# Sparse attention with a gated convolution: the same operations of one TensorE-bound kernel in another fixed order

## Chip, cores and metric

The kernel runs on 1 core of one Trainium2 chip. The metric is the time of one execution on the device in microseconds (us), the median of several runs. A core has five engines, each with its own instruction stream that it works off strictly in order: TensorE (PE in the profile; its weight loads are PEld), VectorE (DVE), ScalarE (ACT), GpSimd (POOL) and SyncE (SP). Here SyncE issues all DMAs. The engines meet through semaphores alone: an instruction waits until what it reads is written, and until what it overwrites has been read.

## The reference, cut to what matters

There are 8 batches of 8 heads with 576 tokens and head width 64. Heads 0 to 3 attend locally (the 32 tokens up to their own), heads 4 to 7 to every 32nd token up to their own. The result, 512 wide per token, goes through a gated projection.

```python
scores = q @ k.T / 8                       # per batch and head
rel = pos[:, None] - pos[None, :]
mask_local = (rel >= 0) & (rel < 32)                          # heads 0..3
mask_strided = (rel >= 0) & (pos[None, :] % 32 == pos[:, None] % 32)   # heads 4..7
attn = softmax(where(mask, scores, -1e9));  x = attn @ v      # x: (8, 576, 512)
gate = sigmoid(sum(conv_w[k] * shifted(x, 4 - k) for k in range(5)))
out = (gate * (x @ w_val)) @ w_out
```

## The kernel before, in words

Each batch b goes through these steps; their names are those of the groups in the code.

* **L b.u** (u = 0, 1, 2), local attention of a third of the tokens: scores on TensorE into a bank of `s_ps` (two banks), maximum and subtraction on VectorE, the exponential on ScalarE, the sum and its reciprocal on VectorE, the product with the reciprocal on GpSimd into `PB`, transposes on TensorE into `t_ps` (one bank), three or more copies on ScalarE into the block-diagonal tile `BDL` (two buffers), and the *value product* with V (`vLs`) on TensorE into `x_ps` (two banks). ScalarE copies it out rounded as `xhi` and whole as `xs`, and VectorE makes `xlo`, what the rounding left.
* **S b.u** (u = 0, 1), strided attention in the same way with `KBS`, `qSs`, `SMS`, `PS`; VectorE transposes into `PT`, four ScalarE copies fill `BDS` (one buffer), and two value products use `vSs`.
* **G b.e** (e = 0 to 3), the gate of 128 columns: a convolution of five taps. For batch 0 and e = 0, 1 it is a convolution on TensorE with diagonal weights that GpSimd writes into `ghi` and `glo` from `cws`; else four instructions on VectorE between two on ScalarE.
* **V b.e**, the value: twelve matmuls of 128 x 512 (a product of w_val's and x's high and low parts) into a bank of `m_ps` (three banks). For batch 0 they come in two halves of six: the first half uses rows 0 and 1 of w_val and the local x alone, the second half rows 2 and 3 and the strided x. VectorE multiplies by the gate into `GV`, ScalarE rounds to `ghi`, GpSimd makes `glo`.
* **P b.m** (m = 0 to 3), the projection by w_out: twelve matmuls that need all four e, a ScalarE copy, the store.

w_val and w_out come as 64-bit floats, in four row blocks each (0 to 3). *Making* a row block is a load (512 KB), a conversion on ScalarE, two instructions on VectorE, the rounding cast on ScalarE (the high part) and a subtraction on GpSimd (the low part). Some tiles are zeroed first; V for the strided heads, `vSs`, has an instruction of its own on VectorE for it, and its loads wait for that.

Tiles are allocated by hand and the scheduler of the framework is off. `plan.add` numbers the steps as they are written, and `plan.issue` (line 53 of the profile; nearly every instruction carries that line) issues them in the order of the string `SEQUENCE`. The numbers of the steps that matter here: 36 zeroes `vSs`; 44, 50, 56, 62 load w_val's rows, 183, 189, 195, 201 w_out's; 82 to 86 load batch 0's strided V; 100, 118, 134 are the value products of L0.0, L0.1, L0.2 and 152, 156, 174, 178 those of S0; 209 and 213 are the TensorE convolutions of G0.0 and G0.1; 227 and 228, 232 and 233, 237 and 238, 242 and 243 are the halves of V0.0, V0.1, V0.2 and V0.3; 247 is P0.0's matmuls; 263 and 264 load batch 1's local V (its first part of 96 rows, then the rest); 287 is L1.0's value product. A token such as `f0x6` issues six matmuls of a zeroed tile (`idle`) into an unused bank, here called idle matmuls.

Of the kernel before, what the change touches and what calls it, by code (L numbers as in the profile page):

```python
# [549 lines left out]
f0x6 f0x4 f0x3 f0x6 44 0 1 32 73 71 37 22 74 72 2 18 3 75 7 46 45 8 5 38 9 33 35 47 183 10 17 11 23 76 48 4 12 21 6 50  # L550
29 20 27 13 56 24 34 81 25 14 49 87 16 31 78 15 39 88 80 105 26 89 62 90 106 f0x1 79 40 91 41 107 121 77 92 189 122
185 51 259 93 123 94 262 52 19 95 57 261 108 96 f0x3 f0x1 f0x1 53 184 260 58 109 54 186 30 55 110 187 124 97 111 28
113 64 63 112 59 99 42 138 125 207 65 98 139 160 f0x3 43 140 188 141 126 142 114 f0x2 60 143 127 115 36 100 116 128
190 129 161 f0x1 101 61 117 144 66 84 102 103 104 130 162 145 195 118 131 163 133 212 83 191 132 70 85 134 211 192 82
291 135 146 86 136 67 147 119 274 f0x1 f0x1 193 266 137 120 164 201 194 213 148 275 268 165 69 267 196 166 276 265 149
197 151 277 150 208 198 278 156 279 167 152 68 168 292 308 153 280 199 293 282 423 209 169 157 281 158 425 154 200 309
173 171 310 202 159 294 155 172 203 170 311 295 178 296 174 204 179 325 312 269 297 180 298 283 175 424 181 176 227
299 326 221 422 182 177 327 284 263 285 222 328 286 228 215 264 313 210 223 214 300 216 329 347 f1x1 303 314 205 224
# [89 lines left out]
```

## Time and profile before

| | |
|---|---|
| median of 3 runs | 313.57 us (313.2 to 314.05) |
| the profiled execution | 315.54 us, of which the span from first to last instruction is 313.5 us |
| busy in the span | PE 298.1 us (95%), PEld 238.4, DVE 230.7 (74%), ACT 217.6 (69%), POOL 149.9 (48%) |
| mean granted TensorE clock | 0.988 of full speed |
| chain that ended last | PE 78%, ACT 6%, DVE 4%, DMA 4%, POOL 3% |

The profile is of one execution. Times in it count from the span's first instruction. "Busy" is the time in which an engine has an instruction running; a line of the timeline gives the start, the time for all instructions merged into it, engine, operation, the tile written and those read, their shape and count, and in brackets how long the engine was idle before it and what ended that. The chain of waits is followed back from the last instruction. Overlapping instructions of one engine make durations add up to a little more than the time that passes.

### The profile page before, as it was taken

The page shows a single profiled execution, that of the slowest core. Times are in us where ns is not written, and L with a number is a line of the kernel's source. Part 1 is how long each engine was busy: PE and PEld are TensorE (multiplying, and loading weights), DVE is VectorE, ACT ScalarE, POOL GpSimd, SP SyncE. Part 2 cuts the span into 40 slices and gives each one's busy share as a digit, 9 for nine tenths or more (in the row PEclk, how much of TensorE's full clock was granted, in tenths as well). Part 3 has the DMA queues.
Part 4 walks back from the last instruction along what each step waited for, and adds up shares of the span by engine and source line. Part 5 has one row for each costly group of instructions (what it writes and reads, how often), then busy time and mean ns, then how long its engine had stood idle before and what let it go on. Part 6 is the DMA issues. An engine that isn't in the chain of part 4 may idle for free.

```text
span 313.5 us, 10550 instructions
## 1 busy us (share of the span) xinstructions
PE 298.1 (95%) x4418; PEld 238.4 (76%) x4421; DVE 230.7 (74%) x435; ACT 217.6 (69%) x499; POOL 149.9 (48%) x204
## 2 busy tenths in 40 slices
PE   7577998999999999999999999999999999999994
PEld 2345886888888888888887888878877888878873
DVE  5698978798788997989675887598688479258500
ACT  7568684997587959978597698778894864542421
POOL 8369848386447742684256346603441280520410
PEclk9959999999999999999999999999999999999999
DMA  7985747647672646466074126041303001001014
GB/s 245 384 326 152 256 128 250 181 127 240 215 232 75 220 146 210 150 192 225 35 233 140 69 92 226 2 151 38 107 0 120 33 34 69 36 33 67 33 43 93
DMA packets 20383, 43.96 MB, mean 140 GB/s; under 512 B 3120, under 2 KB 9008, under 8 KB 19760
## 3 DMA queue, kind: packets, MB, share of 16 engines
q1 hardware_dynamic: 20336, 43.28, 42.6%
q8 instruction: 35, 0.57, 0.8%
q14 instruction: 12, 0.10, 0.1%
HBM read 33.84 MB, written 9.44 MB: 138 GB/s over the span
## 4 chain that ended last, share of the span: by engine, by line
PE 78%; ACT 6%; DVE 4%; DMA 4%; POOL 3%; issue 2%; SPq 1%; POOLq 0%; DVEq 0%; ACTq 0%
PE m_ps L53 58%; PE x_ps L53 11%; PE s_ps L53 7%; PE t_ps L53 3%; DMA vLs<-in_vL_dram 2%; DMA KBL<-in_kL_dram 2%; POOL glo L53 2%; DVE gate L53 1%; ACT BDL L53 1%; ACT xhi L53 1%; DVE GV L53 1%; SPq L53 1%; POOL xlo L53 1%; ACT gate L53 1%; ACT ghi L53 1%
## 5 line engine op out<-in xcount | busy, mean ns | idle before, releaser
L53 DVE SCALAR_TENSOR_TENSOR gate<-xs,cw,gate 128x512 f32<-128x512 f32 x120 | 91.7, 787 | 8.5 <-ACT gate L53 8.0
L53 PE MATMUL m_ps<-xhi,wv 128*128 128x512 f32 x288 | 90.5, 396 | 0.0
L53 PE MATMUL m_ps<-wo,ghi 128*128 128x512 f32 x256 | 80.3, 395 | 0.0
L53 PEld LDWEIGHTS m_ps<-xhi,wv 128*128 128x128 f32 x288 | 53.1, 188 | 11.2 <-issue 0.4
L53 POOL TENSOR_TENSOR glo<-GV,ghi 128x512 fp32r<-128x512 f32 x32 | 42.1, 1320 | 35.7 <-ACT ghi L53 32.6
L53 PE MATMUL m_ps<-xlo,wv 128*128 128x512 f32 x144 | 56.3, 391 | 0.0
L53 PEld LDWEIGHTS m_ps<-wo,ghi 128*128 128x128 f32 x256 | 47.2, 188 | 9.7
L53 POOL TENSOR_TENSOR PB<-SML,ST 128x256 f32<-128x256 f32 (+1 forms) x48 | 28.3, 605 | 52.9 <-DVE ST L53 45.0
L53 PE MATMUL m_ps<-wo,glo 128*128 128x512 f32 x128 | 50.2, 392 | 0.6 <-POOL glo L53 0.6
L53 DVE SCALAR_TENSOR_TENSOR GV<-gate,m_ps 128x512 f32<-128x512 f32 x36 | 24.3, 681 | 21.2 <-PE m_ps L53 11.6
L53 ACT COPY BDL<-t_ps 32x128 f32<-32x128 f32 (+2 forms) x108 | 34.2, 318 | 3.1 <-PE t_ps L53 1.6
L53 DVE TENSOR_TENSOR xlo<-x_ps,xhi 128x256 fp32r<-128x256 f32 (+1 forms) x56 | 24.7, 452 | 14.9 <-ACT xs L53 8.7
L53 ACT COPY BDS<-PT 32x288 f32<-32x288 f32 x64 | 27.6, 432 | 8.6 <-PE x_ps L53 4.2
L53 ACT ACTIVATE osb<-m_ps 128x512 f32<-128x512 f32 (+1 forms) x36 | 21.2, 592 | 16.2 <-PE m_ps L53 12.8
L53 PEld LDWEIGHTS m_ps<-xlo,wv 128*128 128x128 f32 x144 | 27.0, 188 | 5.8
L53 ACT CAST xhi<-x_ps 128x256 fp32r<-128x256 f32 (+1 forms) x56 | 22.3, 403 | 11.3 <-PE x_ps L53 11.0
L53 PEld LDWEIGHTS m_ps<-wo,glo 128*128 128x128 f32 x128 | 24.0, 188 | 6.5 <-POOL glo L53 1.4
L53 ACT COPY xs<-x_ps 128x288 f32<-128x288 f32 (+1 forms) x53 | 22.1, 429 | 9.7 <-PE x_ps L53 9.4
L53 DVE TENSOR_REDUCE ST<-SML 128x6 f32<-128x390 f32 (+1 forms) x45 | 24.2, 546 | 5.8 <-ACT SML L53 5.4
L53 ACT ACTIVATE gate<-gate 128x512 f32<-128x512 f32 x34 | 21.2, 630 | 8.4 <-DVE gate L53 8.1
L53 ACT CAST ghi<-GV 128x512 fp32r<-128x512 f32 x32 | 19.5, 619 | 10.6 <-DVE GV L53 10.4
L53 POOL TENSOR_TENSOR PS<-SMS,ST 128x256 f32<-128x256 f32 (+1 forms) x32 | 16.0, 514 | 20.3 <-DVE ST L53 20.3
(113 smaller groups left out, 443.2 us busy)
## 6 DMA issues: line engine op xcount, KB each, us to landing
out_dram<-osb SPq DMA_DIRECT2D x32, 256.0 KB, 2.3
vLs<-in_vL_dram SPq DMA_DIRECT2D x8, 640.0 KB, 5.2
qLs<-in_qL_dram SPq DMA_DIRECT2D x16, 288.0 KB, 3.5
KBL<-in_kL_dram SPq DMA_DIRECT2D x16, 288.0 KB, 4.1
KBS<-in_kS_dram SPq DMA_DIRECT2D x16, 288.0 KB, 4.9
qSs<-in_qS_dram SPq DMA_DIRECT2D x16, 288.0 KB, 4.6
vSs<-in_vS_dram SPq DMA_DIRECT2D x32, 128.0 KB, 3.6
raw<-in_w_val_dram SPq DMA_DIRECT2D x2, 512.0 KB, 4.8
```

The costliest lines, as they stand in the source:

```text
L53: fn(**kw)
```

## The change

Only the string `SEQUENCE` differs: the same 1497 steps, each once, in another order, and 22 idle matmuls in place of 34. Engine by engine, in the part before P0.0:

* **VectorE.** Zeroing `vSs` moves from behind L0.2's reciprocal to the third place of all. Of the weight conversions only w_val row 0 stays in front; row 1 comes behind L0.2's subtraction, w_val rows 2 and 3 and all of w_out's behind more steps of batch 0's attention.
* **ScalarE.** Zeroing of `BDL` and `PB` moves ahead of the first exponential. Conversions of w_val rows 2 and 3 and of w_out go behind L0's and S0's attention steps.
* **SyncE.** Batch 0's strided q and K go out directly behind the local ones, then conv_w, w_val row 1, the first part of local V, w_out row 0, a K half of batch 1, the rest of local V, the rest of batch 1's local q and K, one load of strided V, the first part of batch 1's local V (263), and only then w_val row 3, w_out row 1, the rest of batch 0's strided V, w_val row 2 and w_out row 2.
* **TensorE.** Before: L0's scores; L0.0's transposes; S0's scores; the rest of L0 up to its value products; L1.1 and L1.0's scores; G0.1; value products of S0.0; L1.2's scores; G0.0; value products of S0.1; S1.0's scores; L1.0's transposes; V0.0; L1.1's transposes; S1.1's scores; first half of V0.1; L2.0 and L2.1's scores; L1.2's transposes; L1.0 and L1.1's value products; L2.2's scores; second half of V0.1, first half of V0.3; L1.2's value product; S2.0's scores; L2.0's transposes; V0.2; second half of V0.3; S1.0's products; S2.1, L3.0's scores; L2.1's transposes; L3.1 and L3.2's scores; S1.1's products; P0.0. After: L0's and S0's scores between L0's transposes and value products, with all of L1's scores; first half of V0.0; G0.1; S0.0's products; G0.0; S0.1's products; L1.0's transposes; V0.2; second half of V0.0; V0.1; L1.1's transposes; S1's scores; V0.3; L2.0's scores; L1.0's value product; L2.1 and L2.2's scores; L1.2's transposes; two idle matmuls; L1.1's value product; S2.0's scores; L1.2's value product; P0.0.
* **GpSimd.** The low parts of the weights go behind attention steps in the same way; the low parts of V0's product come earlier.

From there on the two orders differ by less and less, to about 160 us; behind that they are one. The beginning of the diff:

```diff
--- before.py
+++ after.py
 SEQUENCE = """
-f0x6 f0x4 f0x3 f0x6 44 0 1 32 73 71 37 22 74 72 2 18 3 75 7 46 45 8 5 38 9 33 35 47 183 10 17 11 23 76 48 4 12 21 6 50
-29 20 27 13 56 24 34 81 25 14 49 87 16 31 78 15 39 88 80 105 26 89 62 90 106 f0x1 79 40 91 41 107 121 77 92 189 122
-185 51 259 93 123 94 262 52 19 95 57 261 108 96 f0x3 f0x1 f0x1 53 184 260 58 109 54 186 30 55 110 187 124 97 111 28
-113 64 63 112 59 99 42 138 125 207 65 98 139 160 f0x3 43 140 188 141 126 142 114 f0x2 60 143 127 115 36 100 116 128
-190 129 161 f0x1 101 61 117 144 66 84 102 103 104 130 162 145 195 118 131 163 133 212 83 191 132 70 85 134 211 192 82
-291 135 146 86 136 67 147 119 274 f0x1 f0x1 193 266 137 120 164 201 194 213 148 275 268 165 69 267 196 166 276 265 149
-197 151 277 150 208 198 278 156 279 167 152 68 168 292 308 153 280 199 293 282 423 209 169 157 281 158 425 154 200 309
-173 171 310 202 159 294 155 172 203 170 311 295 178 296 174 204 179 325 312 269 297 180 298 283 175 424 181 176 227
-299 326 221 422 182 177 327 284 263 285 222 328 286 228 215 264 313 210 223 214 300 216 329 347 f1x1 303 314 205 224
-315 431 232 302 348 301 430 330 316 349 429 206 437 229 428 454 438 350 317 439 351 287 225 440 304 331 288 455 289
-471 352 333 320 332 456 306 587 233 217 319 457 230 270 334 441 271 318 242 442 231 305 273 290 458 443 336 459 588
-337 445 321 234 444 272 488 218 323 585 322 446 353 376 219 586 237 370 377 338 447 371 238 448 449 460 235 324 462
-307 220 354 472 243 335 355 239 236 226 489 240 356 339 461 343 473 341 510 372 345 474 340 600 593 511 357 344 342
-463 427 360 601 241 358 617 490 359 346 475 634 244 491 365 373 245 361 464 246 492 602 432 247 362 476 363 436 374
-466 603 382 426 465 477 493 366 591 367 364 478 512 604 433 494 250 388 479 605 594 496 375 368 495 618 592 619 749
-378 750 497 467 606 389 500 450 608 501 251 383 480 607 451 253 248 452 620 249 498 453 751 468 513 635 483 434 482
-384 481 252 514 394 390 435 379 748 380 515 651 516 385 517 484 636 673 395 485 637 499 609 755 469 256 621 756 610
-622 254 590 652 486 391 386 398 653 387 470 654 533 487 623 381 518 624 674 612 519 257 625 611 392 258 506 655 757
-396 534 502 754 763 397 523 504 589 522 406 764 520 765 638 656 503 766 521 639 508 675 767 399 676 507 402 393 657
-505 659 509 400 658 535 401 768 769 640 528 403 641 524 530 407 642 529 626 598 525 526 783 770 599 627 527 628 803
-531 771 629 784 404 613 923 804 408 405 630 805 677 920 545 823 785 752 614 660 786 643 595 536 664 409 410 597 632
-615 921 678 539 616 922 644 546 787 369 596 661 806 551 413 824 547 631 807 645 633 646 663 679 808 681 680 788 845
-825 540 647 552 772 649 416 414 846 809 774 553 415 662 255 648 789 537 773 927 791 775 650 926 538 847 826 776 955
-682 790 541 935 848 665 936 669 542 811 684 557 937 686 670 548 938 411 685 412 667 928 683 810 777 671 753 419 666
...
+f0x18 44 0 1 70 73 37 72 22 17 74 31 36 33 30 3 75 5 9 45 6 23 7 78 34 79 8 46 4 11 10 80 21 47 35 12 68 81 48 25 13
+27 38 24 14 26 16 18 50 20 87 19 15 29 76 88 f0x2 32 183 89 105 90 106 91 121 107 2 92 262 122 108 77 93 40 109 123 94
+138 39 260 28 110 95 139 41 49 259 96 124 42 51 52 261 125 160 140 98 207 83 141 53 142 97 111 126 99 113 184 143 112
+161 211 114 162 144 163 145 127 185 164 100 146 116 129 117 147 128 115 54 43 186 263 130 148 55 101 118 62 131 102
+132 189 119 274 86 133 212 187 275 134 85 120 104 291 82 136 276 135 308 84 71 137 277 165 56 227 64 63 103 188 195
+166 149 292 424 150 213 293 167 190 201 191 294 151 268 65 168 192 66 208 278 169 295 67 152 193 296 156 279 154 194
+153 280 209 170 155 157 297 58 158 298 57 159 299 173 59 282 172 171 197 60 281 196 61 309 178 214 174 310 180 198 283
+311 269 176 179 237 175 271 181 221 177 422 215 222 238 267 202 216 210 266 223 312 228 265 199 217 423 284 224 285
+232 425 229 264 225 230 233 286 218 231 313 300 234 325 303 219 200 235 347 226 326 431 242 348 301 220 327 430 302
+236 239 428 243 203 429 328 314 204 182 437 329 316 287 205 438 315 454 349 288 206 330 240 471 439 289 455 317 f1x2
+587 440 331 244 319 272 320 332 304 290 318 273 441 333 488 350 334 245 270 321 241 442 351 586 306 456 336 427 352
+338 246 247 443 322 353 588 69 305 489 323 585 490 444 335 324 337 445 307 376 457 472 446 370 377 355 343 248 339 458
+473 354 345 510 459 341 474 356 340 594 250 344 342 359 426 460 378 360 462 357 592 358 346 511 491 593 475 447 476
+461 492 361 371 449 600 363 379 448 617 362 601 251 365 372 463 432 367 477 602 366 253 479 466 435 512 478 382 493
+434 603 465 364 464 494 368 249 513 618 604 433 383 496 591 634 619 495 467 373 749 450 468 605 514 384 480 589 388
+256 606 748 451 374 608 481 751 452 515 469 607 497 750 254 620 635 499 436 516 501 385 394 621 517 500 453 482 389
+498 375 636 483 470 637 673 395 651 386 484 756 380 609 252 486 390 485 754 398 396 622 757 638 652 397 487 381 255
+653 611 639 387 518 391 533 763 623 257 399 624 506 519 258 400 654 502 590 674 508 625 655 402 640 755 392 401 503
+523 675 522 764 393 656 504 676 765 507 520 509 406 766 612 505 677 657 403 521 642 539 678 641 610 534 658 404 767
+524 659 407 405 783 660 408 528 679 768 409 626 599 529 784 525 413 769 551 598 785 770 526 535 596 530 369 629 771
+595 545 527 680 627 597 546 628 663 786 823 803 540 613 681 920 531 643 921 615 804 410 645 922 824 644 805 614 923
+787 547 806 616 825 807 548 845 646 552 630 846 647 631 847 632 808 416 661 848 649 633 826 664 788 536 827 662 541
+648 411 650 955 414 537 412 665 927 789 682 791 935 928 790 549 669 753 772 670 926 542 557 667 671 415 553 684 774
+936 666 686 809 937 773 811 538 938 685 419 558 683 810 554 696 939 672 775 668 776 940 828 975 559 697 417 687 1094
+543 777 691 778 689 1092 941 555 792 692 929 561 793 943 956 544 942 752 957 688 560 420 1095 976 849 1093 796 693 958
+795 794 565 562 798 556 698 550 959 690 699 563 797 694 702 564 977 779 960 995 850 924 781 978 829 812 961 421 566
...
```

## Rows read from the trace of the kernel before

**Rows 1.** Windows: stretch, length, busy us (instructions) of PE, PEld, DVE, ACT, POOL, clock.

```profile
0.00:55.00 55.00, 45.14 (x881) 31.33 (x884) 43.11 (x88) 36.51 (x85) 37.74 (x69) 0.94 0.72 248
55.00:100.00 45.00, 44.97 (x882) 37.12 (x882) 38.80 (x81) 35.57 (x85) 25.31 (x35) 1.00 0.61 183
100.00:150.00 50.00, 49.96 (x987) 41.64 (x986) 44.93 (x88) 41.50 (x101) 28.42 (x37) 1.00 0.57 182
150.00:200.00 50.00, 49.98 (x792) 41.28 (x791) 35.34 (x71) 38.71 (x93) 25.67 (x32) 1.00 0.40 125
```

**Rows 2.** Timeline of PE from 8 to 31 us.

```profile
22.82 0.60 PE L164 MATMUL m_ps<-idle 128*128 128x512 bf16 x2
23.34 0.87 PE L53 MATMUL x_ps<-BDL,vLs 128*32 128x96 f32 x32
...
25.81 0.63 PE L53 MATMUL t_ps<-ident,PB 128*128 128x128 f32 x4 [1.16 <-ACT BDL L53]
...
29.98 0.81 PE L53 MATMUL m_ps<-xhi,glo 128*128 128x512 f32 x2
```

**Rows 3.** Chain that ended last, in order of time: start us, us, what.

```profile
3.82 5.32 DMA KBL<-in_kL_dram
...
12.89 0.34 DVE w L53
...
29.48 0.52 ACT wo L53
```

**Rows 4.** Timeline of ACT, the first exponential and wv1's conversion.

```profile
11.63 0.53 ACT L53 ACTIVATE SML<-SML 128x384 f32<-128x384 f32 x1 [2.01 <-DVE SML L53]
12.28 0.67 ACT L53 ACTIVATE gate<-raw 128x512 f32<-128x512 f32 x1
```

**Rows 5.** Timeline of PE from 28 to 75 us.

```profile
35.80 0.84 PE L53 MATMUL s_ps<-KBL,qLs 128*32 128x128 f32 x24
...
43.03 0.71 PE L53 MATMUL m_ps<-xhi,wv 128*128 128x512 f32 x2
...
45.88 0.60 PE L53 MATMUL t_ps<-ident,PB 128*128 128x128 f32 x4
...
51.65 1.18 PE L53 MATMUL x_ps<-BDL,vLs 128*32 128x96 f32 x42 [0.26 <-DMA vLs<-in_vL_dram]
53.97 0.28 PE L53 MATMUL x_ps<-BDL,vLs 128*32 128x96 f32 x3 [1.15 <-issue]
...
59.30 0.66 PE L53 MATMUL t_ps<-ident,PB 128*128 128x128 f32 x4
...
64.08 1.21 PE L53 MATMUL x_ps<-BDS,vSs 128*32 128x72 f32 x64
...
69.66 0.73 PE L53 MATMUL m_ps<-wo,ghi 128*128 128x512 f32 x2
```

**Rows 6.** Timeline of DVE from 3 to 32 us.

```profile
10.44 0.56 DVE L53 TENSOR_REDUCE ST<-s_ps 128x6 f32<-128x384 f32 x1 [3.58 <-PE s_ps L53]
...
20.34 1.25 DVE L53 TENSOR_TENSOR cws<-cw,cws 128x20 fp32r<-128x20 f32 x1
...
23.90 1.76 DVE L175 MEMSET vSs<- 128x2048 f32 x1 [0.38 <-issue]
```

**Rows 7.** Timeline of SyncE's DMA issues from 0 to 60 us.

```profile
15.69 0.87 SPq L53 DMA_DIRECT2D qLs<-in_qL_dram  x1
25.69 0.58 SPq L53 DMA_DIRECT2D vSs<-in_vS_dram  x1
```

**Rows 8.** DMA issues from 26.9 to 28 us: KB each, median us to landing.

```profile
vSs<-in_vS_dram SPq DMA_DIRECT2D x2, 128.0 KB, 3.7
```

**Rows 9.** Windows, the stretch of ScalarE's 72 steps, columns as in rows 1.

```profile
59.50:97.20 37.70, 37.67 (x701) 31.26 (x700) 33.06 (x70) 30.33 (x73) 20.71 (x29) 1.00 0.66 200
```

**Rows 10.** Windows around the fall of the clock, columns as in rows 1.

```profile
12.20:15.50 3.30, 1.65 (x19) 0.85 (x12) 3.30 (x9) 2.43 (x4) 1.19 (x3) 1.00 1.04 420
15.50:22.50 7.00, 5.21 (x138) 3.17 (x137) 6.74 (x13) 4.01 (x11) 5.21 (x5) 0.51 0.98 365
```

61 rows, old and new, of the table SEQUENCE are left out of this document.

## The prediction

> **What bounds the kernel now.** I read the windows first [rows 1]. From 55 to 200 us TensorE is busy in 144.9 of 145 us; before 55 it is in 45.1, some of that with matmuls of the idle tile. So the kernel is a start in which TensorE can't yet work, and then a queue of TensorE work without holes. What comes after some 160 us stands in the same order on every engine in both kernels. The question is how much earlier TensorE's work becomes dense, and whether it stays so.
>
> TensorE's order in time [rows 2] shows the start: up to 29.98, when G0.1 begins, there are short attention steps and waits, the last large one 1.16 us for BDL copies. The chain [rows 3] says what stands behind the waits. From 12.89 to 30 us it runs through VectorE and ScalarE, and twelve of its pieces are no attention but conversions of w_val and w_out, one zeroing and the split of conv_w: 0.34, 0.69, 0.69, 0.62, 0.73, 0.52, 0.68, 1.23, 1.17, 0.52, 0.67 and 0.52 us (the first and the last are in rows 3), together 8.4 us.
>
> **The change, part by part.** Times of the new order are walked by hand from durations of rows: a step starts when its inputs are there and its engine's predecessor is done.
>
> *Loads.* The five loads behind L0.0's scores stay first; the last K half goes out one slot (0.6 us) earlier. It landed at 9.14 [rows 3]; I take scores at 8.6 (8.2 if the slot counts in full and more, 9.3 if the transfers ahead are the limit). L0.1's maximum and subtraction now stand ahead of L0.0's reciprocal on VectorE and take this back: 13.3 us in both.
>
> *What is left on the chain.* From 15 us ScalarE does in the new order: a conversion of wv1 (0.67 [rows 4]), L0.2's exponential (0.53 [rows 4]), three BDL copies (0.37 each) around S0.0's exponential (0.44), wo0's conversion (0.67), S0.1's exponential at 19.75, when VectorE has its input, three BDL copies, wv1's cast (0.62), a BDS copy (0.43), xhi, two BDL copies, xhi, one BDL copy: done at 24.5. BDL is zeroed before 10 us, in the time when ScalarE has nothing to do (2.01 us of idle are left ahead of the first exponential [rows 4]). Conversion that stays in front: 0.67 + 0.67 + 0.62 on ScalarE, 0.68 on VectorE, 0.62 for wo0's cast: 3.3 of the 8.4 us. S0's two exponentials and a BDS copy that now come ahead cost 1.3. So 8.4 - 3.3 - 1.3 = 3.8 us.
> The walk gives nearly the same: L0.0's value product at 19.4 (was 23.34), L0.2's done at 25.4, V0.0's first half at 26.8 after L1.0, L1.1 and L1.2's scores. L1.2's scores (0.8 us [rows 5]) came later before, so that is 26.0 against 29.98: **+4.0 us**. Bounds: 2.5, if VectorE is twice held up as in the 1.25 us that a subtraction of 20 columns takes [rows 6], with some of the walk's steps late too; 5, if the first scores come at 8.2 and nothing waits.
>
> *vSs zeroing first.* 1.76 us of VectorE leave 23.9 us, where it is full, for 3.7, where it waits [rows 6]: the cover is its 3.58 us of idle before the first scores; without that the price is 1.76. In SyncE's queue vSs's first load had stood from 16.6 to 25.69, until that zeroing was done [rows 7]. Another wait takes its place: the first part of batch 1's V must not overwrite vLs before L0.0's value product ends (20.3), and behind it stand w_val row 3, w_out row 1, batch 0's strided V, w_val row 2 and w_out row 2. At 0.6 us an issue the last vSs load goes at 23.9 and lands by 28 (3.7 us each [rows 8]); S0.0's value product asks for it at 32.8. Cover 4.8 us.
>
> *Value of batch 0 forward.* TensorE now does half of V0.0, G0.1, S0.0's products, G0.0, S0.1's products and then V0 whole (11.4 us, four times the 2.85 from 43.03 to 45.88 [rows 5]). That is a cover: before, L1.0's product waited for vLs until 51.65, and the group stood for another 1.15 us with nothing shown [rows 5]. The load still stands behind S0.1's products in SyncE's queue and lands near 49.5, but TensorE comes to it at 52 to 53. Worth 0.26 (the load's wait alone) to 1.4 us, less 0.2 for one more idle matmul (two take 0.60, overlapping [rows 2]). I take the middle, 0.8 - 0.2: **+0.6**.
>
> *Conversions behind it.* The second half of V0.2 needs row blocks 2 and 3 of w_val. Row 2 lands near 29; its five steps stand between attention steps and end on GpSimd at 39.3; TensorE is there at 41.5. Cover 2.2 us. w_out row 3 is ready at 54.8 and asked for at 61.
>
> *New hand-overs.* V0.3 needs V0.0's bank, free at 46, asked for at 49.5. P0.0, at 59.1, needs the last glo at 61.2, and GpSimd has it at 60.6. S1.0's product asks at 62.5 for a BDS copy that ends at 62.65: the first that is late. At P0.0's start the kernel before stood at 69.66 with 6.2 us more of TensorE work done (0.66 from 59.30, 5.58 from 64.08 [rows 5]); the walk leads by 69.66 - 6.2 - 59.1 = 4.4 us. Beyond, ScalarE is the narrow place. Its next 72 steps, to the last BDS copy of S2.1, are 33.7 us of durations (34.3 before), which took 59.2 to 97.2 before, 30.33 of 37.7 us busy [rows 9]. At that pace the new ones end at 59.5 + 38.0 x 33.7 / 34.3 = 96.8; TensorE asks at 95.4. 1.4 us late; VectorE, with 11.3 us idle from 55 to 150 [rows 1], has more room. I charge **-1.2** (bounds 0, and 5 with ScalarE's pace a tenth slower).
>
> *The clock.* The granted clock is 1.2 GHz from 15.5 to 22.5, after a stretch in which TensorE worked 1.65 of 3.3 us at 2.4 GHz [rows 10]. The new order drops 12 of 34 idle matmuls, nearly all between 14 and 30 us, and waits longest from 16.4 to 18.8 and 20.3 to 21.9. So the slow stretch probably falls some us later, over small steps with slack. I charge **-0.3**; bounds 0 and -3.4 (7 us at half speed, as there, all over full work). The Trainium skill (TensorE: Matmul & The Clock Gate, What's actually happening) calls the throttled state the default, which activity lifts; by that the dropped idle matmuls speak against the change, and the sum would have the -3.4. The trace agrees at 15.5 us; that the new start is too thin no run here shows yet.
>
> **The sum.** 4.0 + 0.6 - 1.2 - 0.3 = 3.1 us. The profiled execution took 315.54 (span 313.5 and 2.0 around it) and would take 312.4; the median, 313.57, is 2.0 less than it and becomes 310.5.
>
> **The rivals.**
> 1. *The lead is given back.* Many waits of 0.2 to 1 us on ScalarE and VectorE between 60 and 130 add up to the lead: 313 to 313.8. For it: the first hand-over is late already. Against it: ScalarE had 7.4 us of idle in those 37.7 [rows 9]. Chance 0.10.
> 2. *The clock falls onto the first convolution.* -3.4 in place of -0.3: 313.6. For it: fewer idle matmuls. Against it: from 22 to 26.8 us seven scores, transposes and products run nearly back to back. Chance 0.06.
> 3. *Slower: ScalarE holds TensorE at S2.1's value product.* TensorE is in order, and from P0 on batch 0's ghi casts and output copies stand among the BDL and BDS copies of batches 1 and 2. If its 72 steps take 15% longer than before, they end at 102.4, 7.0 late; the lead of 4.4 at P0.0 is gone and 2.6 with it: 316.2. It decides (over 0.9 us slower) from 10% more time than before, when they end 5.3 late. For it: only 1.4 us of that wait are needed to be late at all. Against it: the same steps with more idle before. Chance 0.14.
> 4. *Everything fits.* No new wait, both stalls gone: 5 + 1.4 = 6.4 us, 307.2. Chance 0.12.
>
> **How the numbers follow.** The forecast has 0.58. With rival 4, faster by over 0.3% (0.9 us, about what a measurement of this kernel can tell from no change) has 0.69, a hundredth of it lost to slower ends of the forecast's own. Within 0.3%: rivals 1 and 2, 0.16. Slower: rival 3 and that hundredth, 0.15. The likeliest case's own range is 308.4 to 312. For 8 in 10 the range leaves a tenth on each side: from 307.6, just inside rival 4, to 314.9, which takes in rivals 1 and 2 and rival 3's milder part.
>
> **What would show it.** In the profile after: L0.0's value product before 20.5 us; V0.0's first half between 26 and 27.5 and G0.1 ended by 33.5; no wait for vLs at L1.0's product; P0.0 begun near 59; full clock from 26 on; TensorE's steps beyond 160 us some 3 us earlier than before. Wrong it is if TensorE waits over 1 us before V0.2's second half (w_val row 2 late), if it waits for BDL or BDS copies between 62 and 100 for over 3 us together (rivals 1 and 3), or if 1.2 GHz stands in G0.1 (rival 2).

## The result, and the profile after

| | before | after |
|---|---|---|
| median, first comparison | 313.64 us (313.2 to 314.05, 4 executions) | 310.59 us (308.3 to 313.35, 4 executions) |
| ratio, 95% interval | | 0.987 [0.9836, 0.9904] |
| median, second comparison | 313.94 us (312.35 to 317.12, 29) | 309.61 us (309.01 to 310.24, 6) |
| ratio, 95% interval | | 0.9853 [0.9822, 0.9885] |
| the profiled execution | 315.54 us, span 313.5 us | 308.3 us, span 306.5 us |
| PE busy in the span | 298.1 us (95%) | 293.8 us (96%) |

The change makes the kernel faster, by 3.05 us in the first comparison and 4.33 us in the second; forecast were 3.1 us and 310.5 us. The execution of 313.35 us, over 1.5% above the fastest of its kernel, is left out of the ratio. The two traces must be read with care: the profiled execution of before is 1.9 us slower than its median, that of after 2.3 us faster, so they differ by 7.2 us and not by 3 to 4.

The windows after, columns as in [rows 1]:

```profile
0.00:55.00 55.00, 48.68 (x930) 36.03 (x932) 45.07 (x91) 39.07 (x90) 41.05 (x70) 0.97 0.78 252
55.00:100.00 45.00, 44.59 (x1008) 37.10 (x995) 41.66 (x91) 38.63 (x94) 30.99 (x43) 1.00 0.64 199
100.00:150.00 50.00, 49.58 (x972) 40.73 (x971) 44.04 (x86) 39.42 (x97) 23.48 (x31) 1.00 0.53 169
150.00:200.00 50.00, 50.00 (x695) 41.37 (x697) 35.73 (x70) 40.90 (x98) 25.79 (x31) 1.00 0.39 127
```

In the first 55 us TensorE is busy 48.68 us where it was 45.14 [rows 1]. Behind that it is nearly as full as before (0.4 us less in each of the next two stretches). VectorE, ScalarE and GpSimd do 2.0, 2.6 and 3.3 us more before 55 us and 2.9, 3.1 and 5.7 us more between 55 and 100: work that stood later before.

TensorE's timeline after, from 8 to 65 us:

```profile
8.70 0.86 PE L53 MATMUL s_ps<-KBL,qLs 128*32 128x128 f32 x24 [1.60 <-POOL maskF L53]
...
16.82 0.27 PE L53 MATMUL s_ps<-KBS,qSs 128*32 128x36 f32 x7 [1.28 <-issue]
18.39 0.99 PE L53 MATMUL t_ps<-ident,PB 128*128 128x128 f32 x4 [1.07 <-POOL PB L53]
19.31 1.51 PE L53 MATMUL x_ps<-BDL,vLs 128*32 128x96 f32 x32
...
25.90 0.73 PE L53 MATMUL m_ps<-xhi,wv 128*128 128x512 f32 x2
...
27.39 0.62 PE L53 MATMUL m_ps<-xhi,glo 128*128 128x512 f32 x2
...
31.58 1.21 PE L53 MATMUL x_ps<-BDS,vSs 128*32 128x72 f32 x64
...
37.03 1.21 PE L53 MATMUL x_ps<-BDS,vSs 128*32 128x72 f32 x64
...
50.96 0.84 PE L53 MATMUL x_ps<-BDL,vLs 128*32 128x96 f32 x32
...
56.21 0.74 PE L53 MATMUL m_ps<-wo,ghi 128*128 128x512 f32 x2
...
64.79 0.71 PE L53 MATMUL x_ps<-BDS,vSs 128*32 128x72 f32 x32 [0.41 <-ACT BDS L53]
```

L0.0's value product comes at 19.31 (23.34 in [rows 2]), V0.0's first half at 25.90, G0.1 at 27.39 (29.98 in [rows 2]), L1.0's product at 50.96 without the wait and without the 1.15 us with nothing shown of [rows 5], P0.0 at 56.21 (69.66 in [rows 5]). From 26 us to 200 us TensorE waits twice for longer than 0.2 us: 0.41 us at S1.1's product for BDS copies and 0.42 us at 117.30 for BDL copies.

The windows around the fall of the clock after, to be held against [rows 10]:

```profile
12.20:18.60 6.40, 3.45 (x139) 2.30 (x138) 6.31 (x18) 3.95 (x11) 4.36 (x7) 1.00 0.99 334
18.60:22.00 3.40, 3.19 (x40) 2.25 (x38) 2.58 (x8) 2.66 (x7) 3.33 (x6) 0.50 0.51 174
22.00:26.00 4.00, 3.78 (x138) 3.27 (x137) 2.43 (x6) 3.26 (x10) 2.31 (x4) 1.00 0.94 307
```

The stretch at 1.2 GHz is 3 us later and half as long as in [rows 10], and full clock is back before the first value matmuls. The half length is not the new order's doing: in the second profile of the kernel before, further down, it is 3.4 us as well (20.1 to 23.5).

### The profile page after: what moved, and what is told of

It is laid out like the page before. It is cut to its first block, busy times and chain, and to the rows that moved or that the text cites. A ratio compares the mean times of both kernels' runs of the same rounds, so it can differ in the third digit from the quotient of the medians.

```text
span 306.5 us, 10530 instructions
## 1 busy us (share of the span) xinstructions
PE 293.8 (96%) x4408; PEld 236.6 (77%) x4409; DVE 229.9 (75%) x435; ACT 217.1 (71%) x499; POOL 151.9 (50%) x204
## 4 chain that ended last, share of the span: by engine, by line
PE 78%; ACT 9%; POOL 5%; DVE 4%; issue 3%; POOLq 1%; DVEq 0%; ACTq 0%
PE m_ps L53 57%; PE x_ps L53 10%; PE s_ps L53 7%; PE t_ps L53 3%; ACT BDS L53 2%; POOL glo L53 2%; ACT BDL L53 1%; ACT gate L53 1%; DVE gate L53 1%; ACT ghi L53 1%; ACT xhi L53 1%; POOL maskL L53 1%; DVE GV L53 1%; POOL xlo L53 1%; DVE ST L53 1%
## 5 line engine op out<-in xcount | busy, mean ns | idle before, releaser
L53 POOL TENSOR_TENSOR PB<-SML,ST 128x256 f32<-128x256 f32 (+1 forms) x48 | 27.2, 582 | 50.7 <-DVE ST L53 32.2
L53 POOL TENSOR_TENSOR PS<-SMS,ST 128x256 f32<-128x256 f32 (+1 forms) x32 | 18.4, 587 | 16.4 <-DVE ST L53 10.4
```

The lines of the kernel that those rows point to most:

```text
L53: fn(**kw)
```

## The experiments

The time of "before" beside each was measured with it on the same chip. Diffs show the pieces of `SEQUENCE` at the place. Start times of TensorE's steps in the profiled executions, in us, stand in one table, since most experiments are read from it:

| kernel | L0.0's value product | G0.1 | S0.1's first product | V0.0, second half | P0.0 | P1.3 |
|---|---|---|---|---|---|---|
| before | 23.34 | 29.98 | 40.89 | 44.51 | 69.66 | 119.72 |
| before, second profile | 23.93 | 30.14 | 40.86 | 44.48 | 69.49 | 119.50 |
| value only | 23.64 | 29.91 | 42.36 | 46.75 | 61.96 | 118.04 |
| start only, to G0.1 | 19.42 | 28.02 | 43.84 | 46.32 | 72.25 | 122.20 |
| start only, to S0.1 | 18.97 | 28.83 | 38.48 | 44.24 | 70.44 | 120.41 |
| the same, w_out later | 18.96 | 29.19 | 38.84 | 41.88 | 68.85 | 118.84 |
| after | 19.31 | 27.39 | 37.03 | 41.41 | 56.21 | 112.63 |
| after, second profile | 18.95 | 27.61 | 37.27 | 41.66 | 57.87 | 114.27 |

P1.3 is where both orders have the same work of TensorE behind them; the columns ahead of it are not equal in work (the new order has V0 whole ahead of P0.0 and half of V0.0 ahead of G0.1, for instance).

**The changed kernel a second time.** No edit.

> The changed kernel as it is, a second time. If its two traces' lead of 7.05 us over the kernel before is a difference between executions beside a true gain of 3.1, the median is 310.5 (310 to 311) and a profiled execution near the median has its steps beyond 160 us some 3 to 5 us ahead of the kernel before. If the gain is 5 to 7 and the first median was unlucky: 307 to 308.5.

Median 309.61 us (309.01 to 310.24), between the two that were expected; before 313.94. TensorE's timeline and SyncE's issues of this execution (310.06 us):

```profile
47.76 1.33 PE L53 MATMUL s_ps<-KBS,qSs 128*32 128x36 f32 x128 [1.41 <-DMA KBL<-in_kL_dram]
```

```profile
38.54 1.18 SPq L53 DMA_DIRECT2D vSs<-in_vS_dram  x2
39.77 0.58 SPq L53 DMA_DIRECT2D qLs<-in_qL_dram  x1
40.40 0.59 SPq L53 DMA_DIRECT2D KBS<-in_kS_dram  x1
41.04 1.81 SPq L53 DMA_DIRECT2D qSs<-in_qS_dram  x2
```

S1.0's scores stood 1.41 us for batch 1's strided Q and K, a wait that the first profile hasn't. (They read nothing else; the releaser named is a load of KBL, and in two of the experiments below, where the same wait is 0.84 and 0.99 us, one of qSs.) In the new order three of these four loads stand on SyncE's queue behind strided V's, which waits until S0.1's products are done (37.27 and 1.21 us, so 38.5); before, they went out at 29.55 to 33.1 us. They land about when TensorE asks, so the wait is there in some executions and not in others. This explains most of the 1.76 us between the two profiled executions of after; the rest of the 7.2 us between the first two traces is that of before lying above its median and that of after below. At P1.3 the second pair is 119.50 - 114.27 = 5.2 us apart, for 315.34 - 310.06 = 5.3 us.

**The kernel before a second time.** No edit.

> The kernel before, a second profile. If the waits at L1.0's and L1.1's products (0.26 and 1.15 us, and two products of 1.33 and 2.34 us) belong to every execution, they are there again, and the time is 315 to 316. If they belong to some executions only, they are absent and the time is near the median, 313.5 to 314.2; then the prediction's 0.6 us for them was not there to be had.

315.34 us, again above the median beside it, 314.41 us. TensorE's timeline:

```profile
19.15 0.76 PE L53 MATMUL s_ps<-KBS,qSs 128*32 128x36 f32 x64 [3.96 <-DMA qSs<-in_qS_dram]
...
52.92 0.29 PE L53 MATMUL x_ps<-BDL,vLs 128*32 128x96 f32 x4 [1.55 <-DMA vLs<-in_vL_dram]
```

The wait at L1.0's product is there again (1.55 us). That it is missing in the faster executions can't be said from two profiles that are both above the median. S0.0's scores waited 3.96 us for strided q; in the new order, where that load goes out directly behind the local ones, they start at 13.0 us (13.47 in one profile).

**Value of batch 0 forward alone.** The old order up to G0.1 (step 213), then what is left in the new order:

```diff
-164 201 194 213 148 275 268 165 69 267 196 166
+164 201 194 213 68 263 148 275 276 308 277 165 227 166
```

> The old order up to and with G0.1, then the new order of what is left (batch 0's value before L1.0's product). The prediction's theory: only the stall at L1.0's product goes, 0.6 us, and ScalarE's narrow place behind P0.0 stays as it is: 313.0 us (312.2 to 313.4). Rival: the value forward is worth the 0.26 and 1.15 us of idle there and the two products of batch 1 that took 1.33 and 2.34 us in place of 0.85 each, up to 2.5 us: 311.1. Second rival: the whole gain is this part: 310.6.

313.67 us; before 313.94; ratio 0.9988 [0.9965, 1.0012]. The wait at L1.0's product is gone from the trace, as forecast, and V0 is done before P0.0 at 61.96; yet it brings 0.3 us, within what can't be told from nothing, and the time lies outside the theory's 312.2 to 313.4. Both rivals fall.

**Zeroing strided V first, alone.**

```diff
-73 71 37 22 74 72 2 18
+73 71 37 22 36 74 72 2 18
...
-143 127 115 36 100 116 128
+143 127 115 100 116 128
```

> The kernel before with one step moved: the zeroing of strided V stands third in VectorE's order. The prediction's theory: its 1.2 us piece leaves the chain ahead of G0.1: 312.4 us (311.8 to 313.4). Rival: it costs what it gives, since the first masks on GpSimd take longer beside it and L0.0's scores start later: 313.3 to 313.9.

313.35 us; before 313.94; ratio 0.997 [0.994, 0.9999]. By the medians half of what was expected; the interval, 0 to 1.9 us, takes in the expected 1.2. G0.1 stays at 29.96, but S0.1's first product moves from 40.89 to 40.46. The masks on GpSimd don't eat it: L0.0's scores start at 8.92. TensorE's timeline at L1.0's and L1.1's products:

```profile
50.43 1.53 PE L53 MATMUL x_ps<-BDL,vLs 128*32 128x96 f32 x64
```

In this execution (313.07 us) the old order has no wait there: from S0.1's first product to L1.2's product it takes 15.1 us, against 17.0 and 16.8 in the two profiles of before. If the kernel before always had that wait and this one never, the gain would be about 2 us and not 0.6. So the wait belongs to some executions only, and with the 0.3 us of the experiment above most of the 0.6 us that the prediction priced for it was probably not there to be had in the median.

**The start alone, cut at G0.1.** The new order up to G0.1, then what is left in the old order. What the old order has early (rows of w_val and w_out: 57 to 61, 190 to 193, 196, 197) so comes directly behind 213:

```diff
-424 150 213 293 167 190 201 191 294 151 268 65 168 192 66
+424 150 213 57 58 59 65 60 190 61 66 191 192 67
```

> The new order up to and with G0.1, then the old order of what is left (batch 0's value late again, behind batch 1's scores and products). The prediction's theory: the start's lead of 4.0 us comes from this part alone, the 0.6 us of the vLs stall do not come, and with the value late the narrow place of ScalarE behind P0.0 is as before: 309.5 us (308.7 to 310.5). Rival (the traces of both kernels read as they stand): G0.1 ends 3.2 us earlier with 2.2 us of later work done, 5.4 us: 308.2. Second rival: the lead is a difference between two executions and the gain comes from the value: 312 to 313.5.

317.79 us (five executions at 314.59 to 315.99, seven at 317.71 to 319.87); before 313.94; ratio 1.0088 [1.0056, 1.012]. Slower, where 309.5 was expected. The profiled execution is of the upper group. TensorE's and ScalarE's timelines:

```profile
36.34 2.15 PE L53 MATMUL x_ps<-BDS,vSs 128*32 128x72 f32 x64 [4.06 <-ACT BDS L53]
```

```profile
30.61 0.68 ACT L53 ACTIVATE gate<-xs 128x512 f32<-128x512 f32 x1 [3.09 <-DMA xs<-in_w_val_dram]
...
35.86 0.43 ACT L53 COPY BDS<-PT 32x288 f32<-32x288 f32 x1
```

S0.0's product waits 4.06 us for BDS copies. They stand behind conversions on ScalarE, the first of which waits 3.09 us for w_val's row. Behind the wait the clock is at 1.2 GHz from 34.0 to 40.8 us, over G0.0. The start had 28.02 at G0.1 and lost it all. Two later waits of 0.60 and 0.98 us, at 55.59 and 62.00, are shown with no releaser; they come up again below.

**The start alone, cut at S0.1's products.**

```diff
-309 178 214 174 310 180 198 283 311 269 176 179 237
+309 178 214 174 266 69 267 265 198 199 423 425 200 310 202 203 311 204
```

> As e_start_only, but the new order is kept up to and with S0.1's value product, so that the BDS copies for batch 0's strided products stay ahead of the conversions; the rest in the old order, batch 0's value behind batch 1's scores again. If e_start_only lost its lead only to those copies (TensorE stood 4.06 us at S0.0's product and went to half clock), this gives the start's lead of about 4 us without the value: 309.6 to 310.5. Rival: the value forward is what TensorE does while batch 1's attention is not ready; without it waits open between 38 and 60 us and the lead is gone: 312 or more.

314.48 us (312.76 to 315.96; the profiled execution took 315.91); before 314.02; ratio 1.002 [0.9991, 1.0049]. The rival is right in its number. TensorE's and ScalarE's timelines, and the windows around:

```profile
44.24 1.22 PE L53 MATMUL m_ps<-xhi,wv 128*128 128x512 f32 x2 [3.36 <-ACT xhi L53]
```

```profile
40.05 0.62 ACT L53 CAST wo<-w 128x512 fp32r<-128x512 f32 x1 [1.07 <-DVE w L53]
40.57 0.65 ACT L53 ACTIVATE w<-osb 128x512 f32<-128x512 f32 x1
41.13 0.38 ACT L53 COPY xs<-x_ps 128x288 f32<-128x288 f32 x1
42.82 0.52 ACT L53 ACTIVATE SML<-SML 128x384 f32<-128x384 f32 x1 [1.31 <-POOL SML L53]
43.25 0.35 ACT L53 CAST xhi<-x_ps 128x256 fp32r<-128x256 f32 x1
```

```profile
43.00:49.80 6.80, 5.56 (x75) 4.35 (x77) 5.93 (x14) 5.85 (x15) 3.26 (x5) 0.50 0.31 98
```

S0.1's xhi, which V0.0's second half needs, stands behind w_out's conversions: 3.36 us of wait, then 6.8 us at half clock.

**The same, with six conversion steps of w_out behind S0.1's xhi and xlo.**

```diff
-198 199 423 425 200 310 202 203 311 204 179 325 312 269 180 283 175 181 176 326 221 422 182 177 327 284 285 222 328
+423 425 310 311 179 325 312 269 180 283 175 181 176 326 221 422 182 177 198 199 200 202 203 204 327 284 285 222 328
```

> As e_start_s0 (new order up to S0.1's value product, then the old order, batch 0's value late), but six conversion steps of w_out's rows 2 and 3 (two on ScalarE, three on VectorE, one on GpSimd) stand behind the last xhi and xlo steps of S0.1, near where the changed kernel has them. In e_start_s0 TensorE stood 3.36 us at V0.0's second half for an xhi copy queued behind them, and went to half clock. Theory: the conversions' place holds the lead, and the value's place is worth little: 309.6 to 311. Rival: the value forward is needed as work for TensorE while batch 1's attention is made; without it the wait opens again a little later: 312.5 or more.

314.13 us; before 314.41; ratio 0.9977 [0.9949, 1.0004]. TensorE's timeline:

```profile
41.88 0.73 PE L53 MATMUL m_ps<-xhi,wv 128*128 128x512 f32 x2 [0.65 <-ACT xhi L53]
...
45.29 0.66 PE L53 MATMUL t_ps<-ident,PB 128*128 128x128 f32 x4 [1.64 <-ACT BDL L53]
...
50.23 0.86 PE L53 MATMUL s_ps<-KBL,qLs 128*32 128x128 f32 x24 [1.06 <-DVE SMS L53]
...
57.05 0.87 PE L53 MATMUL x_ps<-BDL,vLs 128*32 128x96 f32 x32 [0.27 <-ACT SML L53]
```

At V0.0's second half 2.6 us of the lead are left (41.88 against 44.51); at P0.0 0.8 us (68.85 against 69.66). In between TensorE comes to L1.1's transposes, L2.1's scores and L1.2's product before ScalarE and VectorE have made them ready and stands 1.64, 1.06 and 0.27 us. ScalarE's timeline ahead of the longest of these waits:

```profile
43.03 0.62 ACT L53 CAST wo<-w 128x512 fp32r<-128x512 f32 x1 [0.59 <-DVE w L53]
43.56 0.66 ACT L53 ACTIVATE w<-osb 128x512 f32<-128x512 f32 x1
44.12 1.11 ACT L53 COPY BDL<-t_ps 64x256 f32<-64x256 f32 x3
```

So it too is a wait behind conversions of w_out. In the changed kernel two conversions also stand ahead of these copies, which come at 42.36, but there TensorE has V0.2, V0.0 and V0.1 to do until 45.50.

**ScalarE given more to do.** In the changed kernel eight ScalarE copies are done twice.

```diff
+AGAIN = "468 452 254 257 396 400 508 503".split()
...
-            for fn, kw in self.steps[int(token)][2]:
+            for fn, kw in self.steps[int(token)][2] * (2 if token in AGAIN else 1):
```

> The changed kernel with eight ScalarE copies between 72 and 88 us done twice (the second writes the same values again), 4.2 us more of ScalarE work ahead of the BDS copies of S2.1. The prediction's step (ScalarE is already 1.4 us late there, whatever is added comes out at the end): 313.8. Rival, from the trace of the changed kernel: ScalarE has some 2.5 us of idle in this stretch and its last BDS copy ends 1.3 us before TensorE asks, so 0 to 1.5 us of the 4.2 are seen: 309.6 to 311.1.

Eight executions at 311.29 to 313.2 us (median 312.36) and four at 316.5 to 318.3, 312.74 in all; before 314.02; ratio 0.9944 [0.9909, 0.9978], from the eight. ScalarE's busy time grew by 3.7 us (220.8 against 217.1) for durations of 4.2. Beside the 309.61 and 309.96 us of the kernels without it, 2.4 to 2.8 us come out in the eight. TensorE's timeline:

```profile
82.34 0.87 PE L56 MATMUL x_ps<-BDL,vLs 128*32 128x96 f32 x32 [0.77 <-ACT BDL L56]
...
89.09 0.73 PE L56 MATMUL m_ps<-xhi,wv 128*128 128x512 f32 x2 [0.74 <-ACT osb L56]
...
95.47 0.71 PE L56 MATMUL x_ps<-BDS,vSs 128*32 128x72 f32 x32 [0.64 <-ACT BDS L56]
```

Between the two expectations: ScalarE has 0.9 to 1.8 us in hand here, not -1.4 and not 2.7 or more. What the other four waited for is open.

**The twelve idle matmuls back.**

```diff
-94 138 39 260 28 110 95 139 41 49 259 96 124 42 51 52 261 125 160 140
+94 f0x2 138 39 260 28 110 95 139 41 49 259 96 124 42 51 52 261 125 f0x2 160 140
...
-143 112 161 211 114 162 144 163 145 127 185 164 100 146
+143 112 f0x1 161 211 f0x4 114 162 144 163 145 127 185 164 f0x1 100 146
...
-186 263 130 148
+186 263 f0x2 130 148
```

> The changed kernel with the twelve dropped idle matmuls put back, in the waits between 12.5 and 21 us (two before S0.0's scores, two and one at S0.1's, four before L0.1's transposes, one before L0.0's product, two before L0.2's transposes). The prediction charged 0.3 us for the clock in the start: with the idle matmuls the half clock of 3.4 us stays away or falls in waits, 309.3 (the clock's part gone) to 309.6. Rival: 12 matmuls of some 0.25 us each stand in front of steps of the chain and cost more than the clock gives: 310 to 311. Second rival (the clock is worth half of the 3.4 us at full work): 308.

309.96 us (308.83 to 311.24); before 314.02; ratio 0.9874 [0.9831, 0.9916]. The windows, the same stretches as after:

```profile
12.20:18.60 6.40, 5.08 (x144) 3.01 (x147) 6.31 (x18) 3.96 (x11) 4.36 (x7) 1.00 0.98 336
18.60:22.00 3.40, 2.98 (x63) 1.85 (x65) 2.58 (x7) 2.91 (x8) 3.33 (x6) 1.00 0.39 131
```

The clock stays at 2.4 GHz through the start. V0.0's first half then begins at 25.43 us, 0.5 to 0.7 us before the changed kernel's 25.90 and 26.10; in the median, which lies between theory and rival, nothing of it can be seen.

**Five loads ahead of strided V's on SyncE's queue**, against the wait of 1.41 us:

```diff
-424 150 213 293 167 190 201 191 294 151 268 65 168 192
+424 150 213 293 167 190 201 191 294 151 65 168 192
...
-311 269 176 179 237 175 271 181 221 177 422 215 222 238 267 202 216 210 266 223 312 228
+311 268 267 266 265 264 269 176 179 237 175 271 181 221 177 422 215 222 238 202 216 210 223 312 228
```

> The changed kernel with five loads of batch 1 (strided Q and K, the rest of local V) moved on SyncE's queue ahead of the first load of batch 1's strided V, which waits for S0.0's value product. Theory: in the changed kernel these loads are issued at 40 to 44.6 us and land about when TensorE asks (S1.0's scores waited 1.41 us in one execution, nothing in the other); issued at 29 to 33 us they are there: 308.2 to 309.0, and no execution near 310. Rival: TensorE's steps behind take up the wait anyway, or the loads now share the DMA engines with the last rows of w_val and w_out: 309.6 or slower. The prediction had no wait there at all: 309.6.

(265 and 264 leave their places further on in the same way.) Median of all twelve 313.82 us, before 314.02; five executions at 308.02 to 310.49 (ratio 0.984 [0.9802, 0.9879] from these alone), seven at 313.65 to 316.01. The profiled execution is of the upper group (313.99 us); TensorE's timeline:

```profile
60.97 0.47 PE L53 MATMUL s_ps<-KBS,qSs 128*32 128x36 f32 x30
65.22 0.51 PE L53 MATMUL s_ps<-KBS,qSs 128*32 128x36 f32 x34 [3.79 <-issue]
```

The wait at S1.0's scores is gone, and none of the three expectations had what came: 3.79 us in the middle of S2.1's scores, for nothing that the profile shows, and the clock at 1.2 GHz from 66.4 to 69.8 us behind it.

**One matmul step moved instead.**

```diff
-232 425 229 264 225 230 233 286 218 231 313 300 234 325 303 219 200 235 347 226 326 431 242 348
+232 425 229 264 225 230 233 286 218 231 313 300 234 242 325 303 219 200 235 347 226 326 431 348
```

> The changed kernel with one step moved: V0.3's first half (1.6 us of TensorE) ahead of S1.0's scores. Theory: S1.0's scores asked for their loads at 46.0 to 46.4 us and waited 0 to 1.41 us; asked 1.6 us later the wait is hidden: 308.4 to 309.2. Rival: S1.0's BDS copies ended only 0.24 us before its value product in the changed kernel, so the wait turns up there: 309.6.

314.42 us (310.72 to 318.1); before 314.41; ratio 0.9966 [0.9931, 1.0] without the four slowest. The wait at S1.0's scores is gone here too, and the same hole has come (TensorE's timeline):

```profile
66.06 0.48 PE L53 MATMUL s_ps<-KBS,qSs 128*32 128x36 f32 x34 [3.34 <-issue]
```

**What the hole waits for.** The DMA queues of 54.6 to 62.8 us (packets, MB, share of 16 engines), first of the kernel with the five loads ahead, then of the changed kernel, then of the one below:

```profile
q1 hardware_dynamic: 1178, 2.16, 83.6%
```

```profile
q1 hardware_dynamic: 1171, 2.14, 83.3%
q8 instruction: 2, 0.03, 1.5%
```

q8 brings blocks of instructions: in the changed kernel 35 of them, 0.57 MB, and 8,817 of the 10,530 instructions are TensorE's matmuls and weight loads. That they are TensorE's shows in the places of the holes: before them the traces record 449 instructions of TensorE (the changed kernel at 16.82), 1,729 and 1,985 (start alone at 55.59 and 62.00), 2,240 (five loads ahead, 65.22) and 2,241 (V0.3's half moved, 66.06). But for one record these are whole multiples of 256 apart, and 35 blocks of about 256 are TensorE's whole stream. In the changed kernel blocks come at 52.80, 57.23 and 62.50 us; with the five loads ahead at 53.61 and then at 62.89, and TensorE goes on 1.4 us after that block has landed. With V0.3's half moved they come at 54.78 and 63.73. So TensorE stood because its next instructions weren't there. The last experiment keeps the five loads ahead and takes one large load (427) away from that stretch:

```diff
-586 306 456 336 427 352 338 246
+586 306 456 336 352 338 246
...
-474 356 340 594 250 344 342
+474 356 340 594 427 250 344 342
```

> As e_loads_first, with one load more moved: the large part of batch 2's local V (640 KB, issued at 56.9 us there) goes out only behind the next strided K load, at about 62 us. In e_loads_first seven of twelve executions took 313.6 us or more, and the profiled one stood 3.8 us at S2.1's scores with nothing shown, until a block of TensorE's own instructions, fetched by DMA, had come at 62.9 to 63.8 us, 9.3 us after the block before it, when the loads issued from 53.4 to 58.7 us were through. Theory: the block is late because of that traffic; a third of it less after 57 us, the wait shrinks to 1.5 us or goes: median 308.4 to 309.5, no execution over 312. Rival: the late block has nothing to do with the loads: again half of the executions at 313 to 316. Third way: batch 2's V now comes too late for L2.1's value product (asked at 71 us): 310 to 312 in all.

310.62 us (308.4 to 312.22, six executions); before 314.3; ratio 0.9874 [0.9829, 0.992]. Its DMA queues in the same stretch, and S2.1's scores:

```profile
q1 hardware_dynamic: 575, 1.67, 63.2%
q8 instruction: 2, 0.03, 1.5%
```

```profile
62.54 0.78 PE L53 MATMUL s_ps<-KBS,qSs 128*32 128x36 f32 x64
```

The block is in time and no execution is in the upper group, six of six where five of twelve were before. That speaks for the traffic as part of the cause; the counts are small. It isn't the whole of it: the changed kernel moves as much (2.14 MB) and gets its blocks, so probably when a block is asked for beside the loads decides as well. The median misses the 308.4 to 309.5 of the theory. No wait for batch 2's V is in the trace, but the clock in its start was low for long (window, columns as in [rows 1]):

```profile
20.20:27.00 6.80, 6.00 (x116) 5.47 (x120) 3.67 (x8) 4.26 (x13) 3.74 (x6) 0.50 0.83 249
```

G0.1 began at 29.36 here. None of these versions beats the changed kernel.

## Why the prediction was right, and which steps were not

The forecast of 310.5 us stands against medians of 310.59 and 309.61, both in the likeliest case's own range of 308.4 to 312. No rival came true. Its steps did less well than its sum, which is in part luck: a start sized about 1 us too small, a wait of 1.4 us at S2.1 that did not come, and waits elsewhere that were not forecast made up for each other.

* **Start, +4.0: right in place, sized too small.** The value product came at 19.31 and 18.95 (19.4 forecast), V0.0's first half at 25.90 and 26.10 (26.8). S0.1's first product is 3.9 and 3.6 us earlier (37.03 against 40.89, 37.27 against 40.86), with V0.0's first half done besides, which took 25.90 to 27.39: 5.1 to 5.4 us, above the upper bound of 5. At the place where the prediction took it, V0.0's first half less 0.8 for L1.2's scores, it is 4.9 and 4.7. That conversions had been what held the start is shown by what happened when they were put ahead again: TensorE stood 4.06 us behind BDS copies and 3.36 us behind xhi.
* **The sum of two parts: the step that failed.** The prediction priced the start (+4.0) and the value forward (+0.6) as terms that add. Neither alone is worth anything that can be told from nothing: the start alone gave 317.79, 314.48 and 314.13 us, the value alone 313.67. Together they are worth 4.3. The best pair of profiles is the start alone with w_out later and the last experiment. Both have 6.8 us at half clock in the start (the last experiment has its loads moved besides). They begin G0.1 at 29.19 and 29.36 and S0.1's first product at 38.84 and 39.02, and they come to P1.3 at 118.84 and 114.53: behind the same start the new order is worth 4.3 us, behind the old start 0.3 in the median. So the two parts need each other; why is in part argued. The reading: a lead is only kept if TensorE finds work where it then arrives early, and this work is batch 0's value. The prediction saw the value as a cover for one load; by this reading it covers L1's and S1's attention between 41 and 57 us. The rival: the start-alone versions also have conversions at other places, and the longest waits of all three (4.06, 3.36 and 1.64 us) stand behind conversions. A version with the value late and every conversion of w_out at its place of the changed kernel would tell the two apart; it wasn't tried.
* **Zeroing first: right.** Its own worth, not priced by itself, is 0.6 us by the medians (0 to 1.9 by the interval).
* **Hand-overs, -1.2: wrong in sign at the place named, right in kind.** ScalarE's last BDS copy of S2.1 was to be 1.4 us late (96.8 against 95.4). It ended at 90.22, and TensorE asked at 91.53: 1.3 us in hand, as in the second profile (91.91 and 93.21), which the doubled copies bear out (0.9 to 1.8 us were swallowed). The walk had made the way from V0.0 to P0.0 32.3 us long; it took 30.3 and 31.8. In its place came 0.41 and 0.42 us elsewhere, and 0 to 1.41 us at S1.0's scores, which the forecast did not have: the loads of strided Q and K of batch 1, moved on SyncE's queue behind one that waits. The part on loads went through batch 0's loads and missed these.
* **Clock, -0.3: right in place, sized too small at G0.1.** The slow stretch fell over small steps, as forecast, but its length differs between executions: 6.8 and 3.4 us in the two profiles of before, 3.4 us in the two of after and 6.8 us in the last experiment. TensorE's order up to G0.1 is the same in after and the last experiment, and with the idle matmuls back but for these. G0.1 began at 26.93 with the idle matmuls and no slow stretch, at 27.39 and 27.61 with 3.4 us of it, at 29.36 with 6.8. In the kernel before it hardly moved (29.98 with 6.8, 30.14 with 3.4). So 0.5 to 2.4 us at G0.1 hang on the clock in the new start, within the bound of 3.4. What is left of it at the end is open: in the medians nothing is (309.96 against 309.61). The rule of the Trainium skill that was cited (TensorE: Matmul & The Clock Gate, What's actually happening) has its direction confirmed: with the idle matmuls back the clock did not fall in the profiled execution.

Added up afterwards with these sizes: 5.2 for the start, 0 to 0.3 for the value itself, less 0.8 for the two hand-overs and 0 to 1.4 at S1.0's scores, is 3.0 to 4.7 us, against the 3.05 and 4.33 measured. Such a sum hides that the start's 5.2 are kept only with the value forward.

## What to carry to other kernels

When an order is changed in two places, price them together: walk the later part with the engine arriving early, and ask of each step there whether its inputs come early too, and what stands ahead of them on their engines. Here three starts that were early at G0.1 lost all or most of their lead by P0.0, behind conversions and attention that was not ready. For each load that changes its place in a queue, look at the instruction ahead of it and what that one waits for. And before explaining a difference between two traces, see how far each execution is from its own median.

## What the runs showed of the hardware that was not expected

TensorE's instructions come by DMA in blocks, 35 in an execution; the profile counts them on the same 16 DMA engines as the data. At 14 to 22 matmuls a microsecond (the windows after) a block lasts some 4 to 9 us, and mostly it is there in time. The Trainium skill says a part of this (Runtime: NRT & Kernel Launch, Instruction fetch mechanics): the sequencer streams them on a queue of its own, and crossing into the next block is mostly hidden. Here it was not always: the waits "issue" of 1.28 us at 16.82 in the changed kernel (block 14.37 to 15.44), of 1.15 us in [rows 5] (block 51.73 to 52.68), and of 3.79 and 3.34 us above each end 1.3 to 1.4 us after a block has landed. With the longest one an execution took 313.99 us, where others of the same kernel took 308 to 310.5; that the other six above 313 had such a hole too is likely, but they were not profiled. Two harmless changes, five loads earlier or 1.6 us of matmuls earlier, were enough to bring them on in the profiled executions. Whether the one execution of 313.35 us of the changed kernel had such a hole is open; it was not profiled.
